# First tile's scaling and split ahead of the first weight's low parts, three weight quarters ahead of two transposes

## The chip, the cores and the metric

The kernel runs on one core of one Trainium2 chip. The metric is the device time of one execution in microseconds (us), and lower is better. The engines are TensorE (PE, with its weight loads as PEld), VectorE (DVE), ScalarE (ACT), GpSimd (POOL), and SyncE (SP), whose queue issues every DMA of this kernel.

## The reference

Block-causal attention (4 batches, 8 heads, 576 positions, head size 64) feeds a dense mixture of 4 experts, and that feeds a second MLP:

```python
scores = scale * np.matmul(q, k.transpose(0, 1, 3, 2))      # masked by blocks of 64
attn = softmax(scores); x = attn @ v                        # 2304 rows of 512
p = domain_probs / (domain_probs.sum(-1, keepdims=True) + 1e-09)
for e in range(E):                                          # 4 experts, 512 -> 1024 -> 512
    h = np.maximum(x @ w1[e], 0.0)
    out += p[:, e:e + 1] * (h @ w2[e])
h = out @ w_in; solu = h * softmax(h); ln = (solu - mu) / sqrt(var + 1e-6) * g_ln
return ln @ w_out
```

## The kernel before

**Number format.** The matmuls of the experts run in 16 bits, and each float32 operand is two 16-bit parts. A scale is taken from sums of squares; the high part is the scaled operand, rounded; the low part is what the rounding left. So a weight goes through this: four DMA loads of 512 KB each into a tile `stage` (two for its halves in later stages), four squares on ACT (`junk<-stage`), a reduce on DVE (`wt` at L215), a matmul with ones on PE (`tp`, L217), a few one-column operations on DVE that end in `ws` (`scale_bits`, L134 to L141), four high parts (POOL at L229 for the first two weights, ACT at L233 later) and four low parts on DVE (L236). The first weight is `w1` of expert 0, the second is `w2` of expert 0.

**Attention.** The 2304 rows are 18 row tiles, t = 0 to 17, of 128 rows. Tiles 0 and 1 have two steps each, and the others have four pairs of heads, p = 0 to 3. A step has the scores on PE (`sps`, L895 or L913), a maximum on DVE (`nm`), an exponential on ACT (`p`, L960), a high part on ACT (L964) and a low part on DVE (L965) into `hl`, a DMA transpose on SP's queue (`pT<-hl`), and the product with the values on PE (`pv`, L995). The score tiles for tile 2 have 192 columns, for tile 3 320, for tile 4 448, for tile 5 twice 288, and for tile 6 192 again. K, Q and V are split into parts on POOL (`ks`, `qhi`, `qlo`, `v`), some low parts on DVE.

**A finished tile.** `finish` has three functions. `rows` writes the normalised rows `xf`. `scale` squares them on ACT (`xh,xt<-xf`) and makes the scale `xs` by three one-column operations on DVE. `split` makes the high part `xh` on ACT (L1048) and the low part on DVE (L1049), issues the transpose `xT<-xh`, and scales the expert weights `pt`. With `xT` of a tile and both parts of `w1`, PE can run the tile's first expert product (`hps`, L373: 96 matmuls of 128 columns per tile in expert 0) and after it the second (`ops`, L395: 24 matmuls of 512 columns per tile).

**What sets the order.** Each engine works through its own queue in order. The code is written out in one order, and a scheduler of the compiler then places the instructions on each engine by that order, by priorities (`high_priority`) and by its own estimate of durations. At the start the written order comes from a string of letters: each letter calls the next function of a list (`w` and `x`: loads of the first and second weight; `W`: squares, scale and splits of the first; `a`, `b`, `c`: scores, probabilities, values of the next step; `f`: the next function of `finish`; `N`, `V`, `S`, `T`, `Z`: K, Q and V work). What a later letter needs is called ahead of it, and what no letter called is called behind the string. From tile 2 on, a planner with fixed costs interleaves attention steps and expert units; it starts from the same state in both kernels. `after(x, y)` places x behind y in the order without a wait of its own. SP's queue holds all DMA issues in the written order.

Of the kernel before, what the change touches and what calls it, by code (L numbers as in the profile page):

```python
# [15 lines left out]
ALU = mybir.AluOpType  # L16
# [45 lines left out]
def tile_kernel(  # L62
# [69 lines left out]
    def scale_bits(T, bits, s, inv):  # L132

        vec.tensor_scalar(  # L134
            out=inv.bitcast(I32), in0=T.bitcast(I32), scalar1=24, scalar2=23,
            op0=ALU.logical_shift_right, op1=ALU.logical_shift_left,
        )
        vec.tensor_scalar(
            out=inv, in0=inv, scalar1=2.0 ** (64 - bits), scalar2=2.0 ** -75, op0=ALU.mult, op1=ALU.max
        )  # L140
        vec.reciprocal(out=s, in_=inv)  # L141

    def after(ins, other):

        tc.add_manual_dep(
            ins.ins, other.ins.name, mybir.DependencyInfo(mybir.DependencyClass.NoSync, mybir.DependencyReason.DATA),
            reason="pace",
        )
# [14 lines left out]
    def paced(ins):  # L163

        if "D" in marks:
            after(ins, marks["D"])
        return ins
# [7 lines left out]
    def w_steps(key, src, bits, inv, tag, load_eng, rows=None, hi_eng=None, place_raw="stage", known=False, less=False):  # L175
# [46 lines left out]
        def split(c):  # L222
            def f():
                m = 512 if less and c < 2 else 1024
                r = stage[key][:, c * 1024:c * 1024 + m]
                hi = wt[key][:, 0].rearrange("p k f -> p (k f)")[:, c * 1024:c * 1024 + m]
                lo = wt[key][:, 1].rearrange("p k f -> p (k f)")[:, c * 1024:c * 1024 + m]
                if hi_eng is gp:
                    h = gp.tensor_scalar(  # L229
                        out=hi, in0=r, scalar1=stage[key, "s"], scalar2=1.0, op0=ALU.mult, op1=ALU.mult  # L230
                    )
                else:
                    h = paced_a(bg_(act.activation(out=hi, in_=r, func=AF.Copy, scale=stage[key, "s"]), "A"))  # L233
                if "last" in stage:
                    after(h, stage["last"])
                stage["last"] = vec.scalar_tensor_tensor(  # L236
                    out=lo, in0=r, scalar=stage[key, "s"], in1=hi, op0=ALU.mult, op1=ALU.subtract
                )
                bg_(stage["last"], "D")
                if "part" in marks:  # L240
                    paced(stage["last"])
            return f

        def place():
# [497 lines left out]
    class Attention:  # L742
# [276 lines left out]
        def finish(self, t):  # L1019
# [22 lines left out]
            def scale():  # L1042
                T = sp.tile([128, 1], F32, tag="xt", name="xt")
                squares(x, T, xh[:, 1].bitcast(BF16))
                scale_bits(T, 4, s, inv)

            def split():
                act.activation(out=xh[:, 0], in_=x, func=AF.Copy, scale=s)  # L1048
                vec.scalar_tensor_tensor(  # L1049
                    out=xh[:, 1], in0=x, scalar=s, in1=xh[:, 0], op0=ALU.mult, op1=ALU.subtract  # L1050
                )
                sync.dma_start_transpose(out=xtile(xT, t, "xT"), in_=xh.rearrange("p a f -> p (a f)"))
                vec.tensor_scalar_mul(pt[:, t, :], pn[:, t, :], inv)

# [230 lines left out]

    ready = {}
    strict[0] = True
    for c in "naSyczZTPPnpwpWbcTZWzxufvWfWPpfzxSTfazSTPwTnbVbyWTapbnwabvvcVPNnVbnVPwxbNuXtPnztzu":
        if c == "f":
            at1.token_f()  # L1290
        elif c in "abc":
            if c == "a" and at1.na < 20 or c == "b" and at1.nb < at1.na or c == "c" and at1.nc < at1.nb:
                getattr(at1, "token_" + c)()
        elif todo[c]:
            token(c)
# [298 lines left out]
```

## Time and profile before

| | us |
|---|---|
| median of 3 runs | 1104.67 |
| lowest and highest of them | 1104.45, 1106.14 |
| profiled execution, its own time | 1104.1 |
| its span | 1102.3 |
| PE busy in it | 1046.6 |
| DVE busy | 797.8 |
| ACT busy | 510.7 |
| POOL busy | 184.7 |

The span is what the trace covers; 1.8 us of the profiled execution lie around it. PE has work for 95% of the span, and POOL works only in its first part. A busy time is a sum over the whole span, and what an engine is worth is read stretch by stretch.

### The profile page before, as it was taken

The numbers are of one execution on the slowest core, as the hardware profiler recorded it, in microseconds if no ns is written. First come the engines' busy times: TensorE is split into PE (matmuls) and PEld (weight loads), VectorE is DVE, ScalarE is ACT, GpSimd is POOL, SyncE is SP. The second block draws the span as 40 slices with busy tenths as digits, with TensorE's granted clock in tenths as the row PEclk, the third lists the DMA queues.
The fourth block names the chain that finished last, engine by engine and source line by source line (L and its number), as shares of the span: only waits on it lengthen the run. The fifth ranks groups of instructions, "written<-read, shape, count | busy, mean of one in ns | idle before, by whom it ended". The sixth has DMA issues, their size and how long they took to land.

```text
span 1102.3 us, 20568 instructions
## 1 busy us (share of the span) xinstructions
PE 1046.6 (95%) x8088; PEld 658.2 (60%) x8088; DVE 797.8 (72%) x1758; ACT 510.7 (46%) x1108; POOL 184.7 (17%) x176
## 2 busy tenths in 40 slices
PE   4488889999999999999999999999999999999998
PEld 4466765556556555655576776766666674444444
DVE  7898787667767766546777656665879558999883
ACT  5667559454765455443353324232346354323222
POOL 4873633334115311000000000000000000000000
PEclk9999999999999999999999999999999999999999
DMA  9877988673896757325431212330244311434333
GB/s 321 228 158 159 251 172 167 162 194 89 191 214 140 172 139 150 59 44 160 139 116 58 77 40 77 115 135 30 96 142 127 106 29 29 96 86 93 71 86 86
DMA packets 225744, 137.95 MB, mean 125 GB/s; under 512 B 184560, under 2 KB 193008, under 8 KB 225648
## 3 DMA queue, kind: packets, MB, share of 16 engines
q1 hardware_dynamic: 225648, 136.65, 49.8%
q8 instruction: 63, 1.03, 0.4%
q14 instruction: 33, 0.27, 0.1%
HBM read 79.47 MB, written 12.06 MB: 83 GB/s over the span
## 4 chain that ended last, share of the span: by engine, by line
PE 76%; DMA 7%; DVE 7%; POOL 5%; issue 3%; ACT 2%; SPq 1%; POOLq 0%; DVEq 0%; ACTq 0%
PE ops L395 30%; PE hps L627 14%; PE hps L373 9%; PE o L1510 8%; PE h L1444 8%; DMA pT<-hl 3%; PE pv L995 2%; PE sps L913 1%; DVE wt L236 1%; PE sps L916 1%; DMA vraw<-in_vC_dram 1%; POOL qlo L793 1%; DVE hch L384 1%; POOL ks L793 1%; POOL v L874 1%
## 5 line engine op out<-in xcount | busy, mean ns | idle before, releaser
L395 PE MATMUL ops<-wt,hch 128*128 128x512 f16 x1728 | 393.9, 380 | 2.5 <-DVE hch L384 1.3
L395 PEld LDWEIGHTS <-hch 128*128 128x128 f16 x1728 | 166.6, 98 | 189.2 <-issue 8.0
L373 PE MATMUL hps<-xT,wt 128*128 128x384 f16 (+1 forms) x1536 | 217.3, 291 | 4.9 <-DVE hch L384 4.6
L373 PEld LDWEIGHTS <-wt 128*128 128x128 f16 x1536 | 127.0, 100 | 65.5 <-issue 9.5
L960 ACT ACTIVATE p<-sps,nm 128x320 f32<-128x320 f32 (+4 forms) x144 | 79.2, 554 | 100.5 <-DVE nm L929 78.7
L965 DVE TENSOR_TENSOR hl<-p,hl 128x320 f16<-128x320 f32 (+4 forms) x132 | 87.1, 677 | 38.9 <-ACT hl L964 38.7
L627 PEld LDWEIGHTS <-S 128*128 128x128 f16 x1152 | 96.0, 98 | 2.8 <-issue 0.7
L1510 PE MATMUL o<-wt,lt 128*128 128x512 f16 (+1 forms) x456 | 95.6, 368 | 0.0
L1444 PE MATMUL h<-wt,x2T 128*128 128x512 f16 x432 | 95.5, 379 | 0.0
L236 DVE SCALAR_TENSOR_TENSOR wt<-stage,ws,wt 128x1024 f16<-128x1024 f32 (+1 forms) x64 | 86.2, 1355 | 6.3 <-ACT wt L233 4.4
L420 DVE SCALAR_TENSOR_TENSOR acc<-ops,coef,acc 128x512 f32<-128x512 f32 x54 | 40.4, 749 | 68.2 <-PE ops L395 68.2
L913 PE MATMUL sps<-ks,qhi 128*128 128x288 f32 (+3 forms) x160 | 68.5, 430 | 14.6 <-ACT p L960 5.2
L627 PE MATMUL hps<-T,S 128*128 128x192 f16 x864 | 76.3, 246 | 0.0
L627 PEld LDWEIGHTS <-wt 128*128 128x128 f16 x864 | 72.8, 98 | 5.8
L640 ACT ACTIVATE stu<-hps 128x384 f32<-128x384 f32 x72 | 34.6, 482 | 86.6 <-PE hps L627 86.4
L1510 PEld LDWEIGHTS <-lt 128*128 128x128 f16 x456 | 44.6, 98 | 48.9
L1444 PEld LDWEIGHTS <-x2T 128*128 128x128 f16 x432 | 42.3, 98 | 51.0
L964 ACT ACTIVATE hl<-p 128x320 f16<-128x320 f32 (+4 forms) x132 | 65.4, 523 | 13.0 <-DMA pT<-hl 12.3
L995 PE MATMUL pv<-v,pT 128*128 128x64 f16 x1392 | 56.5, 196 | 14.2 <-DMA pT<-hl 11.9
L384 DVE SCALAR_TENSOR_TENSOR hch<-hps,hch 128x384 f16<-128x384 f32 (+1 forms) x98 | 52.9, 542 | 21.0 <-ACT hch L383 21.0
L645 ACT ACTIVATE hch<-stc 128x384 f16<-128x384 f32 x72 | 37.4, 521 | 63.7 <-DVE stc L653 63.4
L995 PEld LDWEIGHTS <-pT 128*128 128x128 f16 x1392 | 51.2, 100 | 24.4 <-DMA pT<-hl 14.9
(158 smaller groups left out, 1490.7 us busy)
## 6 DMA issues: line engine op xcount, KB each, us to landing
stage<-in_w_dram SPq DMA_DIRECT2D x50, 512.0 KB, 5.9
raw<-in_qT_dram SPq DMA_DIRECT2D x34, 256.0 KB, 3.3
vraw<-in_vC_dram SPq DMA_DIRECT2D x30, 256.0 KB, 3.0
raw<-in_kT_dram SPq DMA_DIRECT2D x24, 288.0 KB, 3.5
raw<-in_w_dram SPq DMA_DIRECT2D x24, 256.0 KB, 3.5
raw<-in_w_in_dram SPq DMA_DIRECT2D x8, 512.0 KB, 4.9
raw<-in_w_out_dram SPq DMA_DIRECT2D x8, 512.0 KB, 4.2
stage<-wf SPq DMA_DIRECT2D x8, 512.0 KB, 6.3
```

The source lines that it names most:

```text
L236: stage["last"] = vec.scalar_tensor_tensor(out=lo, in0=r, scalar=stage[key, "s"], in1=hi, op0=ALU.mult, op1=ALU.subtract)
L373: pe.matmul(ps[:, j * n:j * n + n], w[:, a, kk, f * 128:(f + 1) * 128], x[:, b * KD + kk, c0:c0 + n], start=(m == 0), stop=(m == 3 * KD - 1),)
L384: marks["D"] = nc.vector.scalar_tensor_tensor(out=h[:, 1, :n], in0=ps[:, :n], scalar=0.0, in1=h[:, 0, :n], op0=ALU.max, op1=ALU.subtract)
L395: pe.matmul(ps, hch[f][:, a, o0:o0 + 128], w[:, b, f, :], start=(m == 0), stop=(m == 3 * KF - 1))
L627: i = pe.matmul(ps[x][:, jj * HT:jj * HT + HT], lhs(a, kk, jj), rhs(b, kk), start=start, stop=(m == 5), skip_group_check=not first or jj > 0,)
L913: pe.matmul(o, q, rhs, start=True, stop=False)
L960: act.activation(out=dst, in_=src, func=AF.Exp, bias=nm[:, j + x:j + x + 1], scale=SCALE, accum_out=sums[:, h:h + 1],)
L964: anc["A"] = act.activation(out=hl[:, c0:c0 + n_], in_=pf[:, 0:n_], func=AF.Copy)
L965: anc["D"] = vec.tensor_tensor(out=hl[:, W + c0:W + c0 + n_], in0=pf[:, 0:n_], in1=hl[:, c0:c0 + n_], op=ALU.subtract)
L995: pe.matmul(o, tt[:, a * nch + c, :], v[:, bb, hs], start=(m == 0), stop=(m == total - 1))
L1444: pe.matmul(ps[:, half], x[:, a * KD + kk, c:c + 128], w[:, b, kk, half * 512:half * 512 + 512], start=(m == 0), stop=(m == 3 * KD - 1),)
L1510: pe.matmul(ps, tt[:, x * KF + f], w[:, y, f, c], start=(m == 0), stop=(m == 3 * KF - 1))
```

## The change

The string of letters is a new one, the high parts of the first two weights on POOL get a high priority and are no longer tied behind the previous low part in the case of the first weight, and two lines tie the first weight's low parts to the first tile: the first of them behind `xs`, the other three behind the tile's own low part `xh`.

```diff
-        vec.reciprocal(out=s, in_=inv)
+        return vec.reciprocal(out=s, in_=inv)
...
                 if hi_eng is gp:
-                    h = gp.tensor_scalar(
-                        out=hi, in0=r, scalar1=stage[key, "s"], scalar2=1.0, op0=ALU.mult, op1=ALU.mult
-                    )
+                    with tc.high_priority(offset=PRI):
+                        h = nc.gpsimd.tensor_scalar(
+                            out=hi, in0=r, scalar1=stage[key, "s"], scalar2=1.0, op0=ALU.mult, op1=ALU.mult
+                        )
...
-                if "last" in stage:
+                if "last" in stage and key != ("w1", 0):
                     after(h, stage["last"])
...
+                if key == ("w1", 0) and "low" in marks:
+                    after(stage["last"], marks["low" if c else "xs"])
...
-                scale_bits(T, 4, s, inv)
+                marks.setdefault("xs", scale_bits(T, 4, s, inv))
...
-                vec.scalar_tensor_tensor(
+                low = vec.scalar_tensor_tensor(
...
+                marks.setdefault("low", low)
...
-    for c in "naSyczZTPPnpwpWbcTZWzxufvWfWPpfzxSTfazSTPwTnbVbyWTapbnwabvvcVPNnVbnVPwxbNuXtPnztzu":
+    for c in "nauSyzzzzZtTpPnwwwwwWbcSSTZWxvWWxTabVvyWxxxabaZZbcfffNVNVVNXWWWWWWNNNNVVVVc":
```

By the rules of the letters, the two strings call the same functions, and both end after the scores of tile 1. Two things stand elsewhere: the last three loads of the second weight are called ahead of the probabilities of tile 1 instead of behind them, and the three functions of tile 0's `finish` ahead of the first weight's splits instead of behind them. The scheduler then places all engines anew. Line numbers behind L229 are 1 to 4 higher in the changed kernel.

On DVE, at the first weight's low parts (`wt<-stage,ws,wt`), with tile 0's scale (`xi`, `xs`) and its low part (`xh`), stands before:

```order
L236 SCALAR_TENSOR_TENSOR wt<-stage,ws,wt 128x1024 x2
L134 TENSOR_SCALAR xi<-xt 128x1
L236 SCALAR_TENSOR_TENSOR wt<-stage,ws,wt 128x1024
L138 TENSOR_SCALAR xi<-xi 128x1
L859 TENSOR_REDUCE vt_452<-vt_308 128x1
L141 RECIPROCAL xs<-xi 128x1
L1053 TENSOR_SCALAR pt<-pn,xi 128x4
L926 TENSOR_REDUCE nm<-sps 128x2
L864 COPY vt_456<-vtp 128x1
L236 SCALAR_TENSOR_TENSOR wt<-stage,ws,wt 128x1024
L1049 SCALAR_TENSOR_TENSOR xh<-xf,xs,xh 128x512
```

and now:

```order
L134 TENSOR_SCALAR xi<-xt 128x1
L138 TENSOR_SCALAR xi<-xi 128x1
L141 RECIPROCAL xs<-xi 128x1
L1057 TENSOR_SCALAR pt<-pn,xi 128x4
L237 SCALAR_TENSOR_TENSOR wt<-stage,ws,wt 128x1024
L1052 SCALAR_TENSOR_TENSOR xh<-xf,xs,xh 128x512
L237 SCALAR_TENSOR_TENSOR wt<-stage,ws,wt 128x1024 x3
L862 TENSOR_REDUCE vt_467<-vt_308 128x1
L929 TENSOR_REDUCE nm<-sps 128x2
L215 TENSOR_REDUCE wt_557<-wt_270 128x1
```

The tile's scale moved ahead of all four low parts and its own low part ahead of three of them; the second weight's reduce (`wt_557`) now follows the maximum of tile 2's third pair.

On SP, at the second weight's quarters (`stage<-in_w_dram 128x2x512`; `128x1024` is the next weight, `w1` of expert 1), stands before:

```order
L92 DMA raw<-in_qT_dram 128x512 x3
L92 DMA raw<-in_kT_dram 128x384 x3
L92 DMA_TRANSPOSE pT<-hl 128x8x128 x2
L92 DMA stage<-in_w_dram 128x2x512 x3
L92 DMA stage<-in_w_dram 128x1024 x2
L92 DMA_TRANSPOSE xT<-xh 128x8x128
L92 DMA_TRANSPOSE pT<-hl 128x6x128
```

and now:

```order
L92 DMA raw<-in_qT_dram 128x512
L92 DMA stage<-in_w_dram 128x2x512 x3
L92 DMA raw<-in_qT_dram 128x512 x2
L92 DMA raw<-in_kT_dram 128x384 x3
L92 DMA_TRANSPOSE pT<-hl 128x8x128 x2
L92 DMA_TRANSPOSE xT<-xh 128x8x128
L92 DMA raw<-in_qT_dram 128x512
L92 DMA stage<-in_w_dram 128x1024 x4
L92 DMA raw<-in_kT_dram 128x384
L92 DMA_TRANSPOSE pT<-hl 128x6x128
```

Three quarters moved ahead of five loads and the two transposes of tile 1's probabilities; tile 0's `xT` is no longer behind any weight; the next weight's four quarters stand together ahead of tile 2's first transpose. Later on the same queue, the four quarters of `w2` of expert 1 stand ahead of three of tile 4's four transposes, where before all of them stood behind all four.

On PE, behind the last scores of tile 2 (`128x192`), where `tp` is the second weight's matmul with ones and `128x320` are the scores of tile 3, stands before:

```order
L918 MATMUL sps<-mc,mr 128x64
L217 MATMUL tp<-wt_557,ones 128x1
L913 MATMUL sps<-ks,qhi 128x320
L916 MATMUL sps<-ks,qlo 128x320
L918 LDWEIGHTS mr
L918 MATMUL sps<-mc,mr 128x64
```

and now:

```order
L921 MATMUL sps<-mc,mr 128x64
L376 LDWEIGHTS wt
L376 MATMUL hps<-xT,wt 128x128
L376 LDWEIGHTS wt
L376 MATMUL hps<-xT,wt 128x128
```

75 first products of tile 0 now stand ahead of tile 3's scores, and `tp` stands earlier, ahead of the last `pv` of tile 1 and of tile 2's last scores. Further on, the expert matmuls that stand ahead of a score in PE's queue are these (`hps` of 128 columns + `ops` of 512 columns):

| ahead of | before | now |
|---|---|---|
| first score of tile 3 | 0 + 0 | 75 + 0 |
| last pair of tile 3 | 130 + 24 | 135 + 24 |
| first score of tile 4 | 131 + 24 | 192 + 26 |
| first score of tile 5 | 197 + 48 | 288 + 68 |
| first score of tile 6 | 384 + 75 | 397 + 96 |
| third pair of tile 7 | 486 + 120 | 480 + 116 |
| first expert unit with 384 columns | 576 + 144 | 576 + 144 |

On POOL the four high parts of the first weight stand in a row instead of with three Q operations between them, and those of the second weight stand four to five places earlier; from the first high part to the last K part of tile 3, the same 37 instructions stand in both queues.

## Rows read from the trace of the kernel before

**Rows 1.** Busy us (instructions) by stage: PE, PEld, DVE, ACT, POOL; clock, DMA share, GB/s.

```profile
0.00:51.00 51.00, 22.91 (x136) 20.30 (x137) 40.03 (x93) 30.76 (x91) 32.87 (x40) 1.00 0.87 274
51.00:75.50 24.50, 21.30 (x238) 16.04 (x237) 23.68 (x41) 12.60 (x38) 23.93 (x20) 0.93 0.65 155
75.50:125.40 49.90, 42.80 (x584) 33.34 (x585) 41.41 (x89) 36.33 (x86) 21.75 (x19) 1.00 0.93 201
125.40:153.00 27.60, 23.37 (x285) 17.06 (x282) 21.65 (x44) 12.92 (x41) 18.78 (x18) 1.00 1.01 223
153.00:178.20 25.20, 21.36 (x263) 16.16 (x260) 16.79 (x38) 20.63 (x56) 6.46 (x6) 0.93 0.79 153
178.20:1102.30 924.10, 914.91 (x6594) 555.28 (x6594) 654.28 (x1457) 397.42 (x800) 80.93 (x74) 1.00 0.43 108
```

**Rows 2.** PE in order of time: start, duration in us; idle before it and releaser.

```profile
39.73 1.44 PE L995 MATMUL pv<-v,pT 128*128 128x64 f16 x24
45.77 0.53 PE L913 MATMUL sps<-ks,qhi 128*128 128x192 f32 x1 [4.60 <-ACT p L960]
...
49.03 0.59 PE L217 MATMUL tp<-wt,ones 128*128 128x1 f32 x2 [1.83 <-DVE wt L215]
...
51.03 2.75 PE L373 MATMUL hps<-xT,wt 128*128 128x128 f16 x24
...
56.15 3.12 PE L373 MATMUL hps<-xT,wt 128*128 128x128 f16 x53
```

**Rows 3.** DVE in order of time, 33 to 46 us.

```profile
33.22 3.68 DVE L236 SCALAR_TENSOR_TENSOR wt<-stage,ws,wt 128x1024 f16<-128x1024 f32 x2
...
39.20 0.16 DVE L141 RECIPROCAL xs<-xi 128x1 f32<-128x1 f32 x1
...
40.70 1.52 DVE L236 SCALAR_TENSOR_TENSOR wt<-stage,ws,wt 128x1024 f16<-128x1024 f32 x1 [0.58 <-POOL wt L229]
42.14 0.98 DVE L1049 SCALAR_TENSOR_TENSOR xh<-xf,xs,xh 128x512 f16<-128x512 f32 x1
...
43.48 1.68 DVE L965 TENSOR_TENSOR hl<-p,hl 128x192 f16<-128x192 f32 x2
```

**Rows 4.** ACT in order of time, 32 to 46 us.

```profile
32.22 0.62 ACT L130 ACTIVATE xh<-xf 128x512 bf16<-128x512 f32 x1
...
39.39 0.72 ACT L1048 ACTIVATE xh<-xf,xs 128x512 f16<-128x512 f32 x1 [4.41 <-DVE xs L141]
...
45.20 0.42 ACT L960 ACTIVATE p<-sps,nm 128x192 f32<-128x192 f32 x1 [0.77 <-DVE hl L965]
```

**Rows 5.** SP's queue in order of time; the duration includes waits inside a group.

```profile
29.60 4.99 SPq L92 DMA_TRANSPOSE pT<-hl  x2
34.64 8.42 SPq L92 DMA_DIRECT2D stage<-in_w_dram  x5
43.16 1.24 SPq L92 DMA_TRANSPOSE xT<-xh  x1
...
110.01 1.56 SPq L92 DMA_DIRECT2D stage<-in_w_dram  x3
...
112.26 9.00 SPq L92 DMA_TRANSPOSE pT<-hl  x2
```

**Rows 6.** POOL in order of time, 30 to 36 us.

```profile
30.54 2.21 POOL L229 TENSOR_SCALAR wt<-stage,ws 128x1024 f16<-128x1024 f32 x2 [3.66 <-DVE ws L141]
...
33.75 2.08 POOL L229 TENSOR_SCALAR wt<-stage,ws 128x1024 f16<-128x1024 f32 x1
```

**Rows 7.** Busy us by stage, one stretch, columns as in rows 1.

```profile
30.50:75.40 44.90, 28.21 (x282) 21.86 (x282) 41.73 (x71) 25.64 (x73) 44.15 (x37) 0.96 0.71 183
```

**Rows 8.** PE in order of time, the last scores of tile 3.

```profile
75.51 0.42 PE L913 MATMUL sps<-ks,qhi 128*128 128x320 f32 x1
```

**Rows 9.** Waits of PE from 75 to 154 us: total us, times, longest.

```profile
PE pv L995 <- DMA pT<-hl: 9.4, 9, 1.7
```

**Rows 10.** PE in order of time, second expert products in a row.

```profile
204.11 6.21 PE L395 MATMUL ops<-wt,hch 128*128 128x512 f16 x28
```

## Prediction

> **What bounds the kernel now.** I read the busy time of each engine by stage first, with cuts where an attention tile hands over or the expert products change shape. From 178.20 us on, PE is busy for 914.91 of 924.10 us [rows 1]: nothing there waits for what the change moves, and both orders have done 576 + 144 expert products when it begins. So the end comes some 924 us behind the moment at which PE gets there, and the question is how much earlier or later than 178.20 that is. The idle time that PE has until then is 28.1 us up to 51.00, 3.2 up to 75.50, 7.1 up to 125.40, 4.2 up to 153.00 and 3.8 up to 178.20 (width less busy, [rows 1]); beside it, two stretches show a mean granted clock of 0.93, 24.5 × 0.07 = 1.7 us short of full speed in each.
>
> Next come the engines that PE waits for. Between 30.50 and 75.40 us POOL is busy for 44.15 of 44.90 us with 37 instructions [rows 7], and the last scores of tile 3 need the last of its K parts and start at 75.51 [rows 8]. That stretch is POOL's. From 125.40 to 153.00 the DMA engines are busy throughout (1.01) and DVE for 21.65 of 27.60 us. In between, PE loses 9.4 us in nine waits for transposes of the probabilities [rows 9].
>
> **Part A, the start of the first expert products (33 to 51 us).** Now DVE starts two low parts at 33.22, and the tile's scale `xs` comes only at 39.20, in the middle of them [rows 3]. ACT, which had ended the squares of the tile at 32.84, waits 4.41 us for it; its high part starts at 39.39 and lasts 0.72 [rows 4]. The tile's own low part starts at 42.14 and lasts 0.98, and SP issues `xT` at 43.16 [rows 3, 5]. In the new order three operations of one column (0.16 each) and `pt` come first: `xs` at 33.22 + 3 × 0.16 = 33.70, the high part by 34.42, one low part (1.84, half of 3.68) by 35.70, the tile's low part by 36.70. `xT` can be issued there, 6.4 us earlier.
>
> This does not move the first expert product by 6.4 us. In PE's queue the product stands behind tile 2's last scores, now at 45.77, whose wait leads through ACT's `p` at 45.20 to DVE's `hl` at 43.48 [rows 2 to 4]. DVE has the same operations to do ahead of that `hl`, so I leave it in place. What PE gets back is the 1.83 us that it waits for the second weight's sum ahead of `tp`, and the 0.59 us of `tp` [rows 2], which falls into the 4.60 us that PE idles ahead of 45.77. That is 2.4 us: the first `hps` at about 48.6 − 1.4 = 47.2, since the first scores of tile 3, which fill the time from 49.62 to 51.03, now stand behind it. Bounds: 1.0 if the weight's sum is late all the same, 4.0 if `hl` too comes earlier.
>
> The three quarters of the second weight that move ahead of tile 1's two transposes are 1.5 MB, 5.7 us at the 274 GB/s of that stage [rows 1]. The transposes, issued at 29.60 now [rows 5], can be late by that much. What covers it: the `pv` that need them start at 39.73 [rows 2]; issue and landing took 4.99 us for the two, so 29.6 + 5.7 + 5.0 = 40.3. I cost it at nothing; without cover it would be 0.6 us. On ACT, the weight's squares find room in the 4.41 us that it no longer waits.
>
> **Part B (51 to 75.5 us).** The gain of A does not last. The last scores of tile 3 wait for POOL's 37 instructions, and the same 37 stand ahead of them in the new order. So 75.5 stays. The expert work ahead of them is 135 + 24 products instead of 130 + 24; at 3.12 us for 53 first products [rows 2] that is 0.3 us more done.
>
> Here a price is missing: what POOL's reordered operations cost beside DVE's. A high part of 1024 columns took 1.10 us (2.21 for two) ahead of DVE's low parts and 2.08 beside them [rows 6], where DVE's took 1.84 instead of 1.52 [rows 3]. Both engines are stretched, neither stops. DVE's low parts are as many as before, so the likely change is nothing; the bounds are one stretched operation fewer (−1.0) and four more, the second weight's high parts (+3.9). The Trainium skill, page "SBUF — State Buffer", section "Who interferes with whom", is harsher: a DVE instruction with two inputs in SBUF and a GpSimd instruction that reads SBUF exclude each other for a whole instruction. By it each of two newly colliding POOL operations would wait 1.84 us, and the sum below would become −2.3 + 3.7 = +1.4; by two operations stretched as in the rows it would become −2.3 + 2.0 = −0.3. The rows bear it out only in part, since DVE's low part grew by 0.32 us and POOL's by 0.98.
>
> **Part C (75.5 to 125.4 us).** The queue now puts more expert products ahead of attention: 61 + 2 more ahead of tile 4's first score, 91 + 20 ahead of tile 5's, 13 + 21 ahead of tile 6's. At 0.059 us for a first product [rows 2] and 6.21/28 = 0.222 for a second [rows 10] these are 4.0, 9.8 and 5.4 us. PE can only be that far ahead if it fills idle time: 5.4 − 0.3 = 5.1 of the 7.1 us, while waiting for transposes. If it does, tile 6's first score stays where it is. I put it 0.1 us later. Bounds: only 2 of 7.1 are filled (3 us later), or all of them (1.7 us earlier with the work of the new order).
>
> **Part D (125.4 to 153 us).** Ahead of tile 7's third pair stand 480 + 116 products instead of 486 + 120, which is 1.2 us less. Between tile 6's first score and there, PE so has 5.4 + 1.2 = 6.6 us less to do: 23.37 − 6.6 = 16.8 of 27.6 us. PE cannot be the bound. DVE's 21.7 us is the floor, and the DMA engines, busy for all of 27.6 us [rows 1], the ceiling. Transfers that were only in the way (weights in flight stretched over the stage) would shrink, the transposes would not; I have no row that parts them and take the middle, 24.6. **Gain 3.0 us**, with bounds 0 and 5.9.
>
> **Part E (153 to 178.2 us).** The 1.2 us that D did not do is done here; there are 3.8 us of idle time, and I let half of it fall there: **+0.6**. The slow level of the clock stays as it is.
>
> **Sum.** 0.1 − 3.0 + 0.6 = **−2.3 us** against the profiled execution's own 1104.1 us: 1101.8. The shown median is 0.57 us higher, so the timed kernel should come to about **1102.3**. The smallest difference that a measurement tells from no change is 0.2%, 2.2 us, so this stands on the edge of it.
>
> **Rivals.**
> 1. *All of it is kept.* PE fills the whole 7.1 us in C and DVE is the floor in D: −1.7 − 5.9 + 0.6 = −7.0, about 1097.7. For it speaks that PE's nine waits in those stages are short, at most 1.7 us [rows 9], and expert work now stands ahead of more of them. Against it: the DMA engines are at 0.93 and 1.01 there.
> 2. *The order changes and nothing comes of it.* Stage D stays at 27.6 us, since the DMA engines carry the same bytes: 0.1 + 0.6 = +0.7, about 1105.4. The share of 1.01 speaks for it; against it, 223 GB/s in D is less than the 274 of the first stage [rows 1], so part of that busy time is not bytes.
> 3. *POOL and DVE hold each other up.* Two more of POOL's operations run beside DVE's low parts, at 0.98 us each: 75.5 moves by 2.0, −2.3 + 2.0 = −0.3, about 1104.4.
> 4. *SP's queue holds tile 4's transposes: slower.* The four quarters of `w2` of expert 1 now stand ahead of three of the four. `stage` has one buffer, so the first of them cannot be issued until DVE has made the last low part of the third weight, and that waits for a high part on ACT, behind tile 3's squares. Before, these loads stood at 110.01 behind all of tile 4's [rows 5]. Queued behind the wait are tile 4's transposes, then its `pv`, and with them tile 5's. The longest hold that the queue shows is 9.00 us for two transposes at 112.26 [rows 5]. PE has 5.4 us more expert work for that time; a shorter hold costs nothing, and one of 9.0 costs 3.6 us with no gain in D: about 1108.3.
>
> **How the numbers follow.** My forecast has 0.45: D's middle is a choice, and its own range is 1099.5 to 1105 (D between 22 and 27, C's small shifts). Of that, 0.28 lies below 1102.5 and 0.17 within 0.2%. Rival 1 has 0.16, all faster. Rival 2 has 0.19, of which 0.17 within 0.2% and 0.02 slower. Rival 3 has 0.05, within 0.2%. Rival 4 has 0.15, all slower. Together: faster 0.44, same 0.39, slower 0.17. The range reaches down to 1096.5, below rival 1 by what part A might give beyond its sum, and up to 1107.5, which leaves out the greater part of rival 4.
>
> **What would show it.** A is right if the first `hps` starts near 47 us and `tp` stands ahead of the 24 `pv` or in PE's idle time behind them. B is right if the last scores of tile 3 still start near 75.5. C: tile 6's first score near 125.5, with PE idle for about 2 us between. D: 24 to 25 us from there to tile 7's third pair, with DVE near 90% busy. E: the first product with 384 columns some 2 us earlier, and about 924 us behind it. I am wrong if SP stands for more than 5.4 us at the loads of `w2` of expert 1, around 90 to 100 us, or if D stays at 27 us; and if the part behind the first 384-column product differs by more than 1 us, the method was wrong.

## The result, and the profile after

The changed kernel takes 1110.08 us (median of 7 runs, 1109.08 to 1113.82) against 1104.67 us of the kernel before in the same session (7 runs, 1103.94 to 1108.17). The ratio is **1.0051, with a 95% interval of 1.0032 to 1.0069**: slower, where 1102.3 was forecast, and outside the range. The profiled execution has a time of its own of 1109.09 us and a span of 1107.3, 5.0 more than before.

Busy us by stage of the kernel after, with the cuts and columns of [rows 1]:

```profile
0.00:51.00 51.00, 25.30 (x168) 23.23 (x169) 41.76 (x100) 30.94 (x92) 32.55 (x40) 1.00 0.85 272
51.00:75.50 24.50, 18.89 (x215) 13.21 (x213) 22.55 (x33) 11.87 (x33) 22.81 (x20) 0.92 0.73 149
75.50:125.40 49.90, 44.49 (x552) 34.26 (x550) 37.03 (x83) 34.88 (x83) 20.37 (x18) 0.93 0.87 204
125.40:153.00 27.60, 24.16 (x311) 18.16 (x309) 21.45 (x49) 16.02 (x47) 16.30 (x17) 1.00 1.00 197
153.00:178.20 25.20, 19.87 (x231) 15.11 (x230) 16.50 (x33) 18.21 (x49) 5.84 (x7) 0.86 0.96 182
178.20:1102.30 924.10, 913.25 (x6610) 554.50 (x6609) 657.81 (x1465) 399.83 (x805) 83.29 (x76) 1.00 0.43 108
```

PE's idle time moves among the stages (the first loses 2.4 us of it, the second gains 2.4), and the granted clock falls in stages where it did not: 0.93 from 75.50 to 125.40, where [rows 1] have 1.00, and 0.86 instead of 0.93 from 153.00 on. In the third stage DVE does 37.03 us of work and not 41.41, so the attention chain is behind.

PE of the kernel after in order of time (start, duration; idle time before it and releaser), the places that [rows 2 and 8] show of before, and the new waits:

```profile
42.93 0.59 PE L217 MATMUL tp<-wt,ones 128*128 128x1 f32 x2
43.55 1.44 PE L998 MATMUL pv<-v,pT 128*128 128x64 f16 x24
45.74 0.53 PE L916 MATMUL sps<-ks,qhi 128*128 128x192 f32 x1 [0.76 <-ACT p L963]
...
46.99 3.28 PE L376 MATMUL hps<-xT,wt 128*128 128x128 f16 x29
...
57.91 0.69 PE L998 MATMUL pv<-v,pT 128*128 128x64 f16 x12 [2.02 <-DMA pT<-hl]
...
73.94 0.39 PE L916 MATMUL sps<-ks,qhi 128*128 128x320 f32 x1 [1.71 <-POOL ks L794]
...
75.65 0.62 PE L916 MATMUL sps<-ks,qhi 128*128 128x320 f32 x1
...
110.02 1.46 PE L998 MATMUL pv<-v,pT 128*128 128x64 f16 x24 [2.69 <-DMA pT<-hl]
...
156.60 0.52 PE L998 MATMUL pv<-v,pT 128*128 128x64 f16 x12 [3.44 <-DMA pT<-hl]
159.02 1.14 PE L998 MATMUL pv<-v,pT 128*128 128x64 f16 x18 [1.89 <-DMA pT<-hl]
...
182.84 6.01 PE L376 MATMUL hps<-xT,wt 128*128 128x384 f16 x36
...
917.31 30.81 PE L1448 MATMUL h<-wt,x2T 128*128 128x512 f16 x142 [1.77 <-DVE acc L423]
```

The first expert product starts at 46.99 instead of 51.03, and tile 3's last scores at 75.65 (75.51 before). Behind them come waits for transposes of 2.69 us (the longest in [rows 9] is 1.7) and, ahead of and behind the stretch of [rows 9], of 2.02, 3.44 and 1.89 us. The same scores last 0.62 us instead of 0.42. The second MLP's first `h` now has a wait of its own.

Where the 5.0 us are is an identity: span = PE busy + PE idle. Busy grew by 1.0 (1046.6 to 1047.7) and idle by 4.0 (55.7 to 59.6). Of the idle time 1.6 stand ahead of 190 us, 1.8 at the wait of `h`, and the rest, 0.6, are small waits. Of the busy time, the slow level of the clock costs 7.3 us against 5.0 before (PE busy × (1 − granted clock), summed over windows of 2 us), so 2.3 us more. That is more than busy grew by, and the other 1.3 us I cannot assign.

### The profile page after: what moved, and what is told of

Same layout as the page of the kernel before. It is cut to its first block, busy times and chain, and to the rows that moved or that the text cites. A ratio compares the mean times of both kernels' runs of the same rounds, so it can differ in the third digit from the quotient of the medians.

```text
span 1107.3 us, 20569 instructions
## 1 busy us (share of the span) xinstructions
PE 1047.7 (95%) x8088; PEld 659.8 (60%) x8088; DVE 797.1 (72%) x1758; ACT 512.2 (46%) x1108; POOL 181.2 (16%) x176
## 4 chain that ended last, share of the span: by engine, by line
PE 77%; DVE 8%; DMA 7%; POOL 3%; ACT 2%; issue 2%; SPq 0%; DVEq 0%; POOLq 0%; ACTq 0%
PE ops L398 30%; PE hps L630 14%; PE hps L376 10%; PE h L1448 8%; PE o L1514 8%; DMA pT<-hl 4%; PE pv L998 2%; DVE wt L237 2%; PE sps L916 2%; PE sps L919 1%; DVE hl L968 1%; DVE hch L387 1%; DMA x2T<-xh 1%; DMA near<-in_kT_dram 1%; DMA vraw<-in_vC_dram 1%
## 5 line engine op out<-in xcount | busy, mean ns | idle before, releaser
L967 ACT ACTIVATE hl<-p 128x320 f16<-128x320 f32 (+4 forms) x132 | 64.8, 523 | 11.0 <-DMA pT<-hl 10.3
L648 ACT ACTIVATE hch<-stc 128x384 f16<-128x384 f32 x72 | 37.4, 521 | 63.5 <-DVE stc L656 63.2
```

What stands on the lines that cost most here:

```text
L967: anc["A"] = act.activation(out=hl[:, c0:c0 + n_], in_=pf[:, 0:n_], func=AF.Copy)
```

## The experiments

I weighed four theories. **S**: SP's queue holds tile 4's transposes behind the loads of `w2` of expert 1 (rival 4). **P**: too many expert products stand ahead of attention's scores on PE, or too few behind. **B**: a PSUM bank that the change shifts puts the last sum of the experts where the second MLP's first tile lies. **O**: no single edit, but the order that the scheduler chooses anew.

The table is the summary to come back to. The ratio is that to the kernel before on the same chip. "Lost to 190" is worked out from one profiled execution of each, in 2 us windows up to 190 us: width less PE busy, plus PE busy × (1 − granted clock). That execution can lie up to 4 us off the median of its runs (a_psh: 1112.86 against 1108.92).

| run | ratio [95%] | lost to 190, us (idle + slow clock) |
|---|---|---|
| kernel before | 1 | 46.5 + 5.0 |
| kernel after | 1.0051 [1.0032, 1.0069] | 48.1 + 7.3 |
| b_psv | 1.0004 [0.9989, 1.0020] | 46.5 + 4.4 |
| a_psh | 1.0033 [1.0017, 1.0048] | 49.0 + 9.6 |
| b_str | 1.0079 [1.0058, 1.0099] | 53.8 + 7.9 |
| b_body | 1.0041 [1.0024, 1.0059] | 50.1 + 7.5 |
| a_x | 1.0066 [1.0044, 1.0087] | 52.1 + 5.8 |
| a_late | 1.0134 [1.0112, 1.0156] | 56.8 + 6.7 |
| a_tie5 | 1.0083 [1.0060, 1.0106] | 54.0 + 7.3 |
| a_tie25 | 1.0089 [1.0063, 1.0116] | 52.3 + 7.2 |
| h51 | 1.0011 [0.9992, 1.0029] | 46.6 + 4.1 |
| h51p | 1.0015 [0.9997, 1.0032] | 49.7 + 3.3 |
| h76 | 1.0019 [1.0004, 1.0034] | 46.1 + 8.4 |
| h97p | 1.0057 [1.0038, 1.0077] | 51.6 + 5.4 |
| h126 | 1.0048 [1.0032, 1.0064] | 47.8 + 10.3 |
| h126p | 1.0049 [1.0031, 1.0066] | 46.2 + 11.1 |
| h188 | 1.0035 [1.0021, 1.0050] | 49.3 + 5.8 |
| s126p | 1.0106 [1.0077, 1.0135] | 55.6 + 6.2 |

The four lowest sums (50.7 to 53.0) belong to the four lowest ratios and the highest (63.5) to the highest ratio, so most of the difference is made in these 190 us, as the prediction took it.

### The bank: a_psh and b_psv

The new string calls the first tile's `rows` ahead of V's scale, so that `free` in `v_scale` is true for batch 0 and its `vtp` goes to another pool of PSUM. a_psh is the kernel after with the old pool; b_psv is the kernel before with the new one.

```diff
 # a_psh
-            free = not strict[0] or not self.xps
+            free = key != 0 and (not strict[0] or not self.xps)
 # b_psv
-            free = not strict[0] or not self.xps
+            free = key == 0 or not strict[0] or not self.xps
```

> Changed kernel; only the PSUM tile of the first batch's value sum (vtp) comes from the pool of hps and ops again, as in the kernel before, instead of the pool of pv. All instructions stand in the same order on every engine. Bank theory: taking that tile from the other pool shifted by one the banks that all later hps and ops use in turn, so that the second MLP's first product needs the bank of the last expert sum; here its wait of 1.8 us near 917 us is gone and the time falls by about 1.9 us, to 1108.2 (about 1.003 of before). Rival, that this wait comes from the order and the late arrival: the wait stays and the time is that of the changed kernel, about 1110.

> Kernel before; only the PSUM tile of the first batch's value sum comes from the pool of pv, as in the changed kernel. Same order on every engine. Bank theory: the second MLP's first product waits about 1.8 us for the last expert sum, as in the changed kernel, though nothing else was changed, and the time rises by about 1.9 us to 1106.6 (1.0017 of before); a little more if tile 1's values wait for the one buffer of that pool near 40 us. Rival: no such wait, 1104.7.

PE, the first `h` of the second MLP, in a_psh and (second fence) the expert product that waits near 540 us there:

```profile
921.10 9.23 PE L1448 MATMUL h<-wt,x2T 128*128 128x512 f16 x42
```

```profile
540.77 3.73 PE L376 MATMUL hps<-xT,wt 128*128 128x384 f16 x12 [3.50 <-DVE hch L387]
```

The wait of 1.77 us at `h` is gone in a_psh and does not come in b_psv. The built programs give the banks, which no trace names: `h` begins with banks 2 and 3, and the experts' last sum is in bank 2 in the kernel after (0 before, 1 in a_psh and in b_psv, where I had expected 2). Over all runs the wait stands in the kernel after, b_str, a_x, h126 and h188 and in no other, and for a_x, h51, h126, h188 and h126p the bank told it ahead. The other half of the theory, that this is worth its 1.8 us, is not shown: a_psh is 0.0018 below the kernel after with overlapping intervals, and its wait near 540 us is 3.50 us (2.08 in the kernel after), with 12 products taking 3.73 us instead of 2.11 behind it.

### Half of the change: b_str, b_body and a_x

b_str is the kernel before with the new string alone, b_body that with all of the rest alone (of which the two ties of the low parts find nothing to tie to under the old string), and a_x the kernel after with the second weight's last three loads behind tile 1's probabilities again.

```diff
 # b_str
-    for c in "naSyczZTPPnpwpWbcTZWzxufvWfWPpfzxSTfazSTPwTnbVbyWTapbnwabvvcVPNnVbnVPwxbNuXtPnztzu":
+    for c in "nauSyzzzzZtTpPnwwwwwWbcSSTZWxvWWxTabVvyWxxxabaZZbcfffNVNVVNXWWWWWWNNNNVVVVc":
 # a_x
-    for c in "nauSyzzzzZtTpPnwwwwwWbcSSTZWxvWWxTabVvyWxxxabaZZbcfffNVNVVNXWWWWWWNNNNVVVVc":
+    for c in "nauSyzzzzZtTpPnwwwwwWbcSSTZWxvWWxTabVvyWabaZZbxxxcfffNVNVVNXWWWWWWNNNNVVVVc":
 # b_body
-                    h = gp.tensor_scalar(
...
+                    with tc.high_priority(offset=PRI):
+                        h = nc.gpsimd.tensor_scalar(
...
-                if "last" in stage:
+                if "last" in stage and key != ("w1", 0):
```

> Kernel before with the new string alone; the high parts of the weights keep their old priority and place and the low parts are not tied to the first tile. If the string alone makes the loss, the time is that of the changed kernel, about 1110; if the ties and the priority make it, it is 1104.7 plus the 1.9 us of the bank, about 1106.6. The order on SP's queue has all four loads of w2 of expert 1 in another place too, so the theory of SP's queue expects its waits for stage to tell which.

> Kernel before with its old string, and only the high priority and the untied high parts on POOL (with the old string the two new ties of the low parts find nothing to tie to). Expert products ahead of tile 5's first score are 202 + 48, nearly as before (197 + 48). Theory of the expert work put ahead: no loss from it, so within 2 us of the kernel before, 1103 to 1107. Rival, that the new priority on POOL makes the loss of the change: 1108 or more.

> Changed kernel with the three quarters of the second weight called behind tile 1's probabilities again; the rest of the new string and the ties stay. The last sum of the experts again stands in the bank that the second MLP's first product needs, so that wait of 1.8 us stays. From tile 5 on the expert products ahead of each score are the same as in the changed kernel (288 + 68 ahead of tile 5's first). Theory of the expert work put ahead: the same time as the changed kernel within 2 us, 1108 to 1112. Rival, that the three quarters ahead of two transposes are the loss: 1105 to 1107.

All three are slower than before: 1.0079, 1.0041 and 1.0066. The string without the rest is 0.0028 above both together, with intervals that overlap, so there is no good half to keep, and taking the three loads back gives nothing. By its number b_body meets its rival, that the priority alone makes the loss, but b_str has the loss without it. This speaks for O.

### SP's queue: a_late

a_late is a_psh with the four loads of `w2` of expert 1 behind tile 4's last transpose. SP of the kernel after in order of time, and its wait there (total us, times, longest):

```profile
99.11 0.89 SPq L92 DMA_DIRECT2D stage<-in_w_dram  x2
...
102.37 5.13 SPq L92 DMA_TRANSPOSE pT<-hl  x1
```

```profile
SPq L92 <- DVE wt L237: 4.8, 1, 4.8
```

```diff
-                load_eng.dma_start(out=sv[:, c * q:(c + 1) * q, :m], in_=dv[:, c * q:(c + 1) * q, :m])
+                x = load_eng.dma_start(out=sv[:, c * q:(c + 1) * q, :m], in_=dv[:, c * q:(c + 1) * q, :m])
+                if key == ("w2", 1) and "t4" in marks:
+                    after(x, marks["t4"])
```

> Changed kernel with the first batch's value sum in the old pool (as a_psh), and the four loads of w2 of expert 1 placed behind the last transpose of tile 4 on SP's queue, as in the kernel before. Theory of SP's queue (the loads hold tile 4's transposes and then share the DMA engines with them; 4 us lost between the first scores of tiles 5 and 6): the transposes of tile 4 land some 3 us earlier, tile 6's first score comes 3 to 4 us earlier at the same work, and the time falls by 2.5 to 4 us below a_psh, to about 1105. Rival, that those transposes are late because their low parts are late on DVE and the weights' traffic only moves behind tile 4: within 1 us of a_psh, about 1108.

The hold is real, 4.8 us, close to the 5.4 from which rival 4 counted it. Removing it made the kernel slower by another 0.010: 1.0134. The loss sits from 154 to 190 us, where 12.5 us are idle and 3.4 lost to the slow clock (7.1 and 2.5 in the kernel after). But the scheduler moved other instructions as well, so this alone doesn't refute S; s126p below holds them.

### Fewer products ahead of a score: a_tie5 and a_tie25

Both are a_psh with ties on PE: in a_tie5 one expert unit is placed behind tile 5's first scores, so that 192 + 48 products stand ahead of them instead of 288 + 68; in a_tie25 each unit of tiles 2 to 5 stands behind the scores written just ahead of it.

```diff
 # a_tie5, without the line that keeps the mark
+                    if m == 0 and e == 0 and t0 == 2 and f == 0:
+                        after(i, marks["sps"])
 # a_tie25
+                    if m == 0 and e == 0 and t0 in (2, 3, 4, 5):
+                        after(i, marks["sps"])
```

> a_psh (changed kernel, first batch's value sum in the old pool), and the first expert products of tile 2 placed on PE behind the first scores of tile 5, so that 192 + 48 products stand ahead of those instead of 288 + 68 (197 + 48 in the kernel before). Theory of the expert work put ahead: the 9.8 us ahead of tile 5's first score push that tile's attention back by 7.9 us and its xT by 12 us, so that tile 5's expert products are missing as filler when PE waits for transposes near 153 to 159 us. Then tile 5's first score comes back to about 97 us here, its xT to 144 to 150 us, PE's idle time between 154 and 190 us falls from some 6 us to about 4, and the time falls by 2 to 4 us below a_psh, to about 1105 to 1107. Rival, that the waits there are the DMA engines' own (transposes landing late whatever PE did before): idle time of 6 us or more stays, and the time is within 1 us of a_psh, 1108.9.

> a_psh with the first expert products of tiles 2 to 5 each placed behind the scores written just ahead of them, so that attention is always ahead: 276 + 50 to 288 + 72 products ahead of tile 5's later scores instead of 379 + 72 to 394 + 96, 300 + 72 ahead of tile 6's first instead of 397 + 96. Theory of the expert work put ahead: attention goes faster up to tile 8 and products are kept for the waits near 153 us; if attention's chain is all that counts, it is faster than a_tie5, 1103 to 1105. Rival, that PE idles for it between 76 and 126 us and nothing fills that: more idle there than 7 us, and 1108 or more.

The longest waits of PE from 50 to 190 us in a_tie25 (total, times, longest):

```profile
PE pv L1000 <- DMA pT<-hl: 13.6, 11, 4.3
PE sps L918 <- ACT p L965: 6.5, 6, 3.5
PE ops L400 <- DVE hch L389: 3.1, 3, 1.9
```

With the products held back, PE only waits for the same attention chain without them: 1.0083 and 1.0089. In a_tie5 tile 5's first score comes at 102.1 (106.5 in a_psh, 104.9 in the kernel after, 97.0 before). So the number of products ahead of a score is not enough to explain the loss. This speaks against P as a theory of PE's queue by itself; here too the scheduler moved other instructions.

### Orders held by hand: h51, h76, h126, h188 and h51p, h97p, h126p, s126p

To take the scheduler out, the order of every engine was written out: that of the kernel after for all that it had started by T, and that of the kernel before for all else, instruction by instruction. T is the number in the name. The code is that of the kernel after; a "p" at the end stands for a_psh's pool.

```diff
-                if strict[0]:
+                if False:
...
+    for text in ORDERS.values():
+        raw = zlib.decompress(base64.b85decode("".join(text)))
+        n, last = 0, None
+        for (d,) in struct.iter_unpack("<h", raw):
+            n += d
+            if last is not None:
+                tc.add_manual_dep(
+                    tc.nc.get_inst_by_name(f"I-{n}"), f"I-{last}",
+                    mybir.DependencyInfo(mybir.DependencyClass.NoSync, mybir.DependencyReason.DATA), reason="pace",
+                )
+            last = n
```

> Held order: on every engine the instructions that the changed kernel had started by 51 us stand first, in its order; all others follow in the order of the kernel before. No scheduler choice is left. Theory of the order behind: the new start costs nothing, and the loss is made by where everything behind it was placed; then the kernel before's time or up to 2 us less, 1102.5 to 1105. The last expert sum stands in another bank than the one that the second MLP's first product needs, so no wait there. Rival, that the new start itself costs (its contention, or the value sum's buffer): 1107 or more.

> Held order, the changed kernel's up to 76 us, the kernel before's behind. Both stood at tile 3's last scores at 75.5 us, with 0.3 us more expert work done in the changed one. Theory of the order behind: as h51, 1102.5 to 1105. Rival, that the loss is made before 76 us by what other engines have not done by then: 1107 or more.

> Held order, the changed kernel's up to 126 us, the kernel before's behind. The last expert sum stands in the bank that the second MLP's first product needs, as in the changed kernel: 1.8 us. Theory of the expert work put ahead: the loss is made between 76 and 126 us, where tile 5's attention is pushed back by 7.9 us and PE runs slow for 3.0 us, and the order behind cannot give it back; 1108 to 1111. Rival, that the order behind 126 us (tile 6's and 7's, with PE's waits of 3.4 and 1.9 us near 156) makes it: 1105 to 1107, which is before's time and the bank.

> Held order, the changed kernel's up to 188 us, the kernel before's behind; the bank as in the changed kernel. All theories: the loss up to the first products with 384 columns (2.8 us) and the bank (1.8 us) are in it, 1108.5 to 1111; a lower time would put loss behind 188 us into the order there.

> Held order, the changed kernel's up to 51 us, the kernel before's behind, and the first batch's value sum in the old pool, so that the last expert sum stands in the same bank as in the kernel before. Theory that the new start is a gain which the order behind it loses: tile 9's scores came 1.0 us earlier in h51 than before, and with the bank of before the wait near 535 us is 2.4 us again and not 3.4 with slow matmuls behind it; 1 us below the kernel before, 1104 to 1105 where that is 1105 to 1106. Rival, that the start is no gain: the same as before or up to 2 us more.

> Held order, the changed kernel's up to 97 us, the kernel before's behind, value sum in the old pool. 249 + 48 expert products ahead of tile 5's first score. Theory that products run early are missing between 55 and 80 us and PE runs slow there: the loss of h76 (1.9 thousandths) is in it and no more, 1107 to 1108.5. Rival, that the loss is made behind 97 us: the time of h51p.

> h126 with the value sum in the old pool, so that the second MLP's first product does not wait. Bank theory: 1.8 us below h126's 4.8 thousandths, that is about 3.2 thousandths over the kernel before, 1108.5 to 1109.5. If the products ahead of tile 5's first score cost, it is 1 to 2 us over h97p; if the loss is all made before 97 us, it is the same as h97p.

s126p is h126p with one thing changed, in SP's order alone: the four loads of `w2` of expert 1 stand behind tile 4's last transpose.

> h126p, with only SP's queue changed: the four loads of w2 of expert 1 stand behind tile 4's last transpose. Theory of SP's queue (the slower rival of the prediction): SP's wait of 4.8 us and the 2 MB in flight hold tile 4's transposes; then PE's wait of 2.7 us for one of them near 108 us, and the slow matmuls behind it, are gone, and the time is 2 to 4 us below h126p. Rival, that the transposes are late because DVE makes the low parts late: the time of h126p within 1 us.

Start of the first scores of a tile, read from PE in order of time in one execution of each:

| | before | h51 | h51p | h76 | h97p | h126 | h126p | h188 | after | s126p |
|---|---|---|---|---|---|---|---|---|---|---|
| tile 4 | 76.8 | 77.0 | 77.0 | 78.8 | 79.5 | 80.5 | 80.7 | 81.2 | 80.5 | 79.7 |
| tile 5 | 97.0 | 97.3 | 97.0 | 98.2 | 104.0 | 104.8 | 105.7 | 105.6 | 104.9 | 106.8 |
| tile 6 | 125.4 | 125.7 | 125.8 | 128.4 | 129.7 | 133.1 | 132.7 | 133.3 | 132.9 | 138.2 |

Busy us from 56 to 80 of the kernels before, after, h51 and h97p, columns as in [rows 1]:

```profile
56.00:80.00 24.00, 19.41 (x218) 13.35 (x215) 22.34 (x40) 15.52 (x45) 20.93 (x18) 0.93 0.67 149
```

```profile
56.00:80.00 24.00, 18.61 (x191) 13.35 (x192) 19.84 (x34) 10.96 (x37) 19.70 (x18) 0.86 0.68 148
```

```profile
56.00:80.00 24.00, 20.12 (x217) 14.97 (x213) 22.36 (x38) 15.32 (x46) 21.17 (x18) 0.90 0.70 153
```

```profile
56.00:80.00 24.00, 16.99 (x200) 11.94 (x200) 19.98 (x34) 11.23 (x39) 19.83 (x18) 1.00 0.63 146
```

PE in h97p, the wait ahead of tile 5's first scores:

```profile
103.19 1.04 PE L998 MATMUL pv<-v,pT 128*128 128x64 f16 x16 [5.32 <-DMA pT<-hl]
104.04 0.59 PE L916 MATMUL sps<-ks,qhi 128*128 128x288 f32 x1
```

Three things follow. The new start alone is worth nothing: 1.0011 and 1.0015, both intervals reach 1. The order up to 76 us costs little (1.0019), although ACT does as little work from 56 to 80 us as in the kernel after (11.0 us, 15.5 before): with the old order behind it, tile 5 is caught up to 98.2. With the new order up to 97 us the whole loss is there (1.0057, against the expectation for h97p), and nothing further is lost behind it (1.0049, 1.0048, 1.0035, 1.0051). And the slow clock is not needed for it: h97p runs at 1.00 from 56 to 80 and has tile 5 at 104.0 all the same, behind a wait of 5.32 us for a transpose.

What stands between 76 and 97 us can be read from the traces. PE at tile 4's third and last pairs of heads, and ACT's first high part of the third weight (`w1` of expert 1), before and (second fence) after:

```profile
90.27 0.45 PE L913 MATMUL sps<-ks,qhi 128*128 128x448 f32 x1
...
92.44 0.56 PE L913 MATMUL sps<-ks,qhi 128*128 128x448 f32 x1
...
98.16 1.15 ACT L233 ACTIVATE wt<-stage,ws 128x1024 f16<-128x1024 f32 x1 [0.93 <-DVE ws L141]
```

```profile
90.57 0.45 PE L916 MATMUL sps<-ks,qhi 128*128 128x448 f32 x1
...
96.87 0.45 PE L916 MATMUL sps<-ks,qhi 128*128 128x448 f32 x1
...
90.17 3.22 ACT L234 ACTIVATE wt<-stage,ws 128x1024 f16<-128x1024 f32 x3
```

At the third pair the two kernels are level, and 4.4 us are lost up to the last one. There ACT now makes three high parts of the third weight in a row, and DVE its low parts (1.27 us each, from 92.43 on); before, both began behind tile 5's first score. In h51, h51p and h76 the first of these high parts starts at 98.06 to 99.36, behind that score, and in h97p, h126, h126p and h188 at 89.65 to 90.81, ahead of tile 4's last pair. So the step of T from 76 to 97, which brings the loss, also moves these splits into tile 4's attention. That they are the cause is argued from this and not shown: no run moves them alone.

Against h126p, s126p is 0.0057 slower with disjoint intervals: the opposite of what S expected. But its edit does not free the transposes. With the four loads gone from their place, SP stands for 6.6 us at the Q load between them, until POOL has made `qlo` (in a_late too), and the last two transposes of tile 4 are issued from 107.78 to 114.64, against 108.91 to 114.10 in h126p. SP's queue in s126p, its wait, and (third fence) in h126p:

```profile
94.18 8.07 SPq L92 DMA_DIRECT2D raw<-in_qT_dram  x2
...
107.78 6.86 SPq L92 DMA_TRANSPOSE pT<-hl  x2
```

```profile
SPq L92 <- POOL qlo L796: 6.6, 1, 6.6
```

```profile
108.91 5.19 SPq L92 DMA_TRANSPOSE pT<-hl  x2
```

So the hold at these four loads does not set when tile 4's transposes are through, and loading `w2` of expert 1 late costs 0.0057. S as the prediction put it, by these loads, is refuted in this order. Whether SP's queue costs something by its other waits, no run tests.

None of the sixteen kernels is faster than the one before, so there is no better version to show.

## Why the prediction was wrong, step by step

The terms of the prediction's sum, from marker to marker in one execution of each kernel:

| part | forecast, us | measured, us | marker at its end: before, after |
|---|---|---|---|
| B | 0 | +0.1 | tile 3's last scores: 75.51, 75.65 |
| C | +0.1 | +7.4 | tile 6's first score: 125.44, 132.95 |
| D | −3.0 | −9.3 | tile 7's third pair: 153.03, 151.28 |
| E | +0.6 | +6.0 | first product with 384 columns: 178.62, 182.84 |
| behind E | 0 | +0.8 | end of the span: 1102.3, 1107.3 |

PE at the markers of C, D and E before, and (second fence) of C and D after:

```profile
125.44 0.34 PE L913 MATMUL sps<-ks,qhi 128*128 128x192 f32 x1
...
153.03 0.39 PE L913 MATMUL sps<-ks,qhi 128*128 128x320 f32 x1
...
178.62 7.47 PE L373 MATMUL hps<-xT,wt 128*128 128x384 f16 x36
```

```profile
132.95 0.33 PE L916 MATMUL sps<-ks,qhi 128*128 128x192 f32 x1
...
151.28 0.41 PE L916 MATMUL sps<-ks,qhi 128*128 128x320 f32 x1
```

C and D miss by 7.3 and 6.3 us in opposite directions, so at the end of D PE stood only 1.2 us behind the forecast (151.28 for 150.1). E misses by 5.4 and makes most of the error.

**Part A was right.** `xs` came at 33.62 (33.70 forecast), `xT` was issued at 37.01 (36.70), tile 2's last scores stayed at 45.74, and the first `hps` started at 46.99 (47.2). `tp` stands in PE's idle time ahead of the 24 `pv`. The three quarters that moved cost tile 1's transposes hardly anything: issued at 29.81, 5.33 us for the two (29.60 and 4.99 in [rows 5]). DVE of the kernel after in order of time:

```profile
33.62 0.16 DVE L141 RECIPROCAL xs<-xi 128x1 f32<-128x1 f32 x1
...
35.47 1.52 DVE L1052 SCALAR_TENSOR_TENSOR xh<-xf,xs,xh 128x512 f16<-128x512 f32 x1
```

**Part B was right.** Tile 3's last scores came at 75.65 for a forecast of 75.5, and rival 3 did not happen. The gain of A was gone by then, as forecast: PE idled 2.02 us at 57.91 and 1.71 at 73.94, and the 2.4 us that the first stage had gained went there. The work done up to the marker is the same, before and (second line) after:

```profile
0.00:75.60 75.60, 44.30 (x373) 36.44 (x373) 63.77 (x134) 43.38 (x129) 56.81 (x59) 0.98 0.80 236
0.00:75.60 75.60, 44.29 (x381) 36.55 (x382) 64.41 (x132) 42.82 (x125) 55.36 (x59) 0.97 0.81 232
```

Four high parts in a row took 5.87 us beside DVE's work, 1.47 each, so they are stretched as in [rows 6]. For the Trainium skill's rule (page "SBUF — State Buffer", section "Who interferes with whom"), by which the two exclude each other for a whole instruction and 75.5 would move by 3.7, no run shows that price. But "neither stops" is not shown either: a longer record can be a wait inside the instruction. And the 1.52 us that the prediction took for DVE's undisturbed low part stood beside POOL's `ks`; with POOL idle the same operation took 1.28 (at 912.27 in the kernel before), so the stretch to 1.84 is 0.56 and not 0.32.

**Part C failed: "PE can only be that far ahead if it fills idle time … 5.1 of the 7.1 us".** Between tile 3's last scores and tile 6's first one PE idled 7.2 us, as before (7.1), where about 2 was forecast: none of it was filled. The slow clock cost 2.8 us there and nothing before. With the 5.1 us of products on top, tile 6's first score came at 132.95 instead of 125.5. I costed the extra products as filler of PE's idle time, and never asked what the new order does to ACT, DVE and the transposes that wait for the scores. Tile 4's first score came 3.8 us late (80.5 for 76.8), which its third pair had caught up, and then its last pair came 4.4 us late, where the third weight's splits now stand. The held orders put the loss into the orders between 76 and 97 us.

**"The slow level of the clock stays as it is" failed too.** The whole span has 2.3 us more of it. Before, the granted clock fell to about 0.55 once ahead of 125 us (62 to 66), and in the kernel after three times, in the windows from 58 to 62, 74 to 80 and 108 to 114, each behind or within one of the new waits of 1.71 to 2.69 us.

**Part D came out with the right sign, and far outside its bounds.** From tile 6's first score to tile 7's third pair (151.28) it took 18.3 us for a forecast of 24.6. It gave back more than C had lost. "DVE's 21.7 us is the floor" was wrong: work that lay in this stretch before now lies ahead of it or behind it.

**Part E failed: "+0.6".** It took 31.6 us instead of 25.6, with 8.0 us idle (3.8 before). At its start PE was 1.8 us earlier than before, with 1.2 us of products less done, but tile 5 was 12.5 us late. SP, tile 5's `xT`, before and (second line) after:

```profile
144.18 1.23 SPq L92 DMA_TRANSPOSE xT<-xh  x1
156.64 1.26 SPq L92 DMA_TRANSPOSE xT<-xh  x1
```

Its products were missing as cover when two waits of 3.44 and 1.89 us for transposes came behind 153 us, and tile 7's last pair came at 159.97 (156.41 before). That the missing products let these waits show is read from the trace. The first product with 384 columns started at 182.84, where some 2 us earlier than 178.62 was forecast. So what C lost in attention was paid here.

**"About 924 us behind it" held in sum: 924.5 for 923.7.** But "nothing there waits for what the change moves" did not. Of the 4.2 us at 182.84, 2.4 are left at 845; then the shift grows to 3.0 at 866 (a wait of 0.71 for ACT) and 5.0 at 917, where `h` waits 1.77 us for the last sum of the experts. The change does reach that place, through the PSUM bank.

**Rival 4 had the sign and not the reason.** The hold was 4.8 us, within the 5.4 that it called free, and s126p shows that tile 4's transposes are not through earlier without it.

**What stays open:** whether the third weight's splits are what makes the loss between 76 and 97 us, since no run moves them alone; whether the bank is worth anything by itself, since a_psh and h126p, which free it, lose some 3 us near 540 us against the kernel after and h126; and 1.3 us between the slow clock's cost and the growth of PE's busy time.

## What to carry to other kernels

Work that is moved ahead fills idle time only once: ask what covers the wait that it used to cover, and what stands behind it on the same engine that other engines wait for. A marker that PE reaches in time (here 151.28 us) says nothing on the work that it does not count (tile 5's `xT`, 12.5 us late), so follow the other engines' chain up to it too. And where a scheduler places everything anew, holding the old order behind a cut, and moving the cut, finds the stretch in which a loss is made better than undoing the edits one by one: each of those kernels was slower than the kernel before. Check also that such an edit frees what it is meant to free: when s126p had moved the loads, another entry of the queue held it for as long or longer (6.6 us for 4.8).

## What the runs showed of the hardware that I had not expected

Waits of 1.7 to 3.5 us can cost a second time. At PE's waits that end at 57.91, 73.94, 110.02 and 156.60, the granted clock went to its lower level (1.2 of 2.4 GHz) within the wait or in the windows of 2 us behind it, and PE's work there took longer. Windows of the kernel after, columns as in [rows 1]:

```profile
56.00:58.00 2.00, 0.09 (x3) 0.10 (x4) 2.00 (x3) 0.49 (x2) 2.00 (x2) 1.00 1.32 126
58.00:60.00 2.00, 2.00 (x19) 1.27 (x19) 2.00 (x3) 0.00 (x0) 2.00 (x2) 0.53 0.29 64
60.00:62.00 2.00, 2.00 (x7) 0.80 (x6) 2.00 (x5) 0.08 (x1) 2.00 (x3) 0.62 0.50 131
62.00:64.00 2.00, 2.00 (x21) 1.33 (x18) 2.00 (x3) 1.61 (x7) 1.82 (x3) 1.00 0.13 26
```

The length of the wait alone does not decide it. Near 535 to 540 us the same 12 products took 2.11 us behind waits of 2.42 (before), 2.08 (after) and 3.32 us (h188), 4.00 us behind 3.12 (b_psv) and 3.37 us (h51), and 3.67 us behind 2.71 (h126p):

```profile
537.77 2.11 PE L376 MATMUL hps<-xT,wt 128*128 128x384 f16 x12 [3.32 <-DVE hch L387]
```

```profile
536.23 4.00 PE L376 MATMUL hps<-xT,wt 128*128 128x384 f16 x12 [3.37 <-DVE hch L387]
```
